# Another tabled order of the instructions of an attention and MoE kernel

## The chip, the core and the metric

The kernel runs on one core of a Trainium2 chip. The metric is the device time of one execution in microseconds (us); less is better. Shown times are of executions without disturbance.

## What is computed

For batch B = 4, heads H = 8, S = 576 positions and head size D = 64, all in float32; `k` and `z_prev` come scaled by 8.

```python
scores = scale * np.matmul(q, k.transpose(0, 1, 3, 2))     # scale = 1/sqrt(D)
scores = np.where(causal, -1000000000.0, scores)
a = np.exp(scores - scores.max(-1, keepdims=True))
a /= a.sum(-1, keepdims=True) + 1e-09
local = np.matmul(a, v)
q_p = phi(q)                      # x + 1 above zero, exp(x) below
mem_out = (q_p @ M_prev) / (q_p . z_prev + 1e-06)
g = 1 / (1 + np.exp(-beta))
x = g * mem_out + (1 - g) * local          # then [2304 tokens, 512]
h = np.maximum(np.maximum(x @ w1, x @ w2), x @ w3)   # [2304, 768]
return h @ w_out                                      # [2304, 512]
```

## The kernel before

The tokens of each batch are cut into two halves, of 320 and 256 rows. A half of a batch with two of its heads is a pair; there are 32 of them, the 16 of the first half first. When the four pairs of a half and batch are done, its tokens go through the MoE part.

For a pair, `load_qk` and `load_v` fetch the inputs (`rk`, `rw` for q and k, `rv` for v, `mv` for the memory). Matmuls take float32 numbers as a high part and a low part in a faster format: `split_q` and `split_k` cast the high part (`qs`, `k` from `rk` or `rw`; on ScalarE or VectorE) and subtract it for the low part (on VectorE or GpSimd). `product` multiplies them on TensorE into one of two PSUM banks, `bs`, which holds one block of scores at a time. `masked` on VectorE reads the bank, adds the causal mask, writes `p` and leaves the least value in `st` (in the trace a CUSTOM_DVE instruction and a read of its accumulator; in the order an ISA instruction); then the bank is free for the next `product`. `exponential` is ScalarE's (`p` from `p` and `st`, sum in `sum`), `turned` makes the reciprocal of the sum on VectorE, `normal` scales `p` on GpSimd. `phi` makes the memory's part (`phe`, `phf`, with the norm `nn`). The blocks of `p` are turned on TensorE into the banks `bt` and copied to `pt` (ScalarE or VectorE) in the first part of the kernel; later VectorE's STREAM_TRANSPOSE turns them in pieces that go to DRAM and come back into `pt` with DMAs. `values` multiplies `pt` with `mv` and `rv` into the bank `bv`, whose result is split into `xh` and `xl`.

`moe_up` multiplies `xh` and `xl` with the three weights' parts `wh`, `wl` into three banks `bm` (three matmuls a product); the greatest of the three is kept in `t` (copy, then VectorE's maxima) and split into `hh` and `hl` (`hhr`, `hlr` for the last 64 of 320 tokens). `moe_down` multiplies with `woh`, `wol`. The weights themselves are split in the first 100 us (`load_weights`: ScalarE, VectorE, and a subtract on GpSimd or VectorE that writes `wl`).

All these instructions are not issued as written but noted in a list, in the order of the program; an instruction that may run on either of two engines is noted with both. `Plan.emit` then issues them in the order that the table `ORDER` gives: each word is a place in the list of what is still to be issued, `b` takes the second engine, and `+n` puts n filler matmuls ahead, which read the mask and write a bank of no use at that time. Each engine runs its own instructions in the order of issue, and waits on others by semaphores that follow from the data. So the table sets what stands in front of what on each of the engines. The table has 5431 words, 13 of them with fillers (119 matmuls) and 205 with `b`. The names in the traces carry L259 (the line in `emit` that issues) for all instructions, and L254 for the fillers.

Of the kernel before, what the change touches and what calls it, by code (L numbers as in the profile page):

```python
# [23 lines left out]
class Half:  # L24
# [27 lines left out]

ORDER = """
    2 0 1 0 0 0 2 15 15 15 4 3 2 1 21+30 22+12 21 21 0 17 15 140 82 10 79 78 77 13 76 6 12 12 18+9 17 17 9 0
    19+10 0 27 0 17 8 6 23 0 16 39+12 5 20 15 34 34 51 33 13 7 34 34 1 0 15 6 2 28 16+6 8 5 5 24 6 2 20 1 0 9
    9 9 31+16 0 8 2 1 3 21 25 106 11+4 1 23 4 9 4 26+2 38 38 8b 1 65 3 23 10 3 1 8 19 7 19 4+6 0 5 3 28 28 50
    8 1 10 2 10 0 31 17 65 14 14 21 63 27 4 4 3 11 57 22 15 23+8 21 30 50 21 143 21 15 11 19 19b 2 21 20 13 18
    39 21 5 2 129 11 11 2 16 17 3 3 5 11 1 11 9 14+1 6 13b 13 0 9 1 109 108 7 18 27 7b 25 8 100 24 0 0 5 21 39  # L60
    5 5 5+3 6 90 5 21 16 0 31 19 1 0 26 25 11 79 2 11 52 14 271 271 0 20 35 36 13 13 8 32 36 17 11 30 31 31 20
    9 3 9 17 25 13 35 16 34 8 16 48 8 20 14 20 8 10 18 7 128 7 10 28 15 125 15 26b 8 19 19 9 18 8 8 58 6 15 3
    34 6 32 15 13 19 49 104 17 28 76 100 0 2 11 11 3 12 3 9 91 26 10 37 25 52 51 9 14 23 17 46 4 184 28 28 22
    2 31 15 39b 3 29 31 19 24 41 17 22 17 6 2 29 29 29 33 32 29 38 37 1 21 14 9 10 132 24b 8 11 23 17 1 8 11 9
    23 23 23 8 11 15 20 50 11 21 133 21b 7 1 9 16 9 16 34 53 23 2 31 121 31 8 8 118 2 16 16 12 14 5 11 27 6
    103 88 4 25 10 9 1 17 50 48 30 31 21 28 44 28 46 22 17 26 3 40 29 29 37b 25 6 19 11 59 17 33 60 32 58 26 1
    11 32 10 69 51 31 21 27 48 28 29 2 82 21 10 25 12 15 10 2 10 20 227 20 20 21 20 37 8 19b 9 12 18 218 31 2
# [3 lines left out]
    31 20 6 28 28 19 27 35 35 35 35 35 35 35 14 34 2 5 12 15 2 19b 1 10 21 25 18 24 7 9 3 17 20 20 62 78 39 20  # L71
    75 75 63 60 61 25 3 24 3 15 22 55 22 22 7 62 65 99 2 97 2 60 1 245 13 58 17 1 1 52 51 15 15 15 15 15 39b
    15 78 77 67 0 66 14 0 72 9 7 16 109 32 62 16 16 65 0 30 7 28 9 74 13 13 13 13 3 12 5 20 1 10 43 10 10 10
    195 78 4 77 9 78 48 48 1b 0b 13 3 19 43 68 0 1 1 70 11 29 65 11 3b 13 13 13 13 13 13 55 13 13 19 9 12 12
    12 24 9 11 72 71 45 72 71 22 31 43b 75 9 16 347 29 29 19 28 1 11 11 8 11 8 133 31 22 22 22 10 12 12 19 19
    19 19 19 14 18 86 40 85b 42 316 40 14 39 39 39 156 115 9 308 16 113 20 13 11 1 11 2 107 5 14 14 68b 10 67
    13 13 46 13 13 134 62 13 85 13 9 6 11 11 8 10 92 10 53 90 76 76 88 53 17 113 80 111 86 0 73 16 82 1b 71 5
    103b 11b 7 0b 76 1 0 1 0 10 10 10 10 10 10 10 10 10 10 10 10 10 117 82 121 115 115 116 10 7 50 113 113 13
    13 13 13 108b 13 13 13 13 3 70 3b 50 0 6 9 38 0 95 8 8 8 63 33 9 8 60 88 89 5 11 3 85 57 64 10 10 26 51 1
    3 4 50 50 22 21 237 237 21 7 7 45 7 7 7 7 7 7 7 7 2 83 83 84 83 159 10 8b 82 0b 80 2 32 32 32 17 17 17 147  # L80
    17 1 7 15 45 1 14 14 14 14 196 9 13 13 13 104 6 148 35 12 8 145 6 139 98 13 10 10 92 7 6 13 13 13 13 4 131
    87 5 1 10 166 10 10 10 10 10 36 76 10 6 9 123 117 122 151 9 34 15 10 14 14 14 14 14 14 14 6 42 13 4 107
    58b 107 5 7 130 1 9 9 55 1 93 8 8 126 122 125 5 2 6 47 11 120 46 84 46b 11 85 4 8 12 12 12 12 12 12 12 12
    12 1 11 11 3 30 10 110 107 108 62 1 107 9 102 102 0 102 94 13 5 12 97 12 12 12 12 93b 95 7 1 93 92 4 4 91
    90 83 83 88 89 88 88 88 4 4 13 47 76 43 43 42 41 36 37 35 37 35 34 34 113 107 113 112 107 105 105 108 112
    112 34 17 17 17 17 17 17 17 104 27 27 57 4 12 25 4 97 57b 57 4 4 4 4 4 4 273 72 132 5 4 130 104 17 17 264
    102 104 252 255 251 21 21 39 3 121 20 1 62 42 36 41 15 71 90 15 17 17 86 143 4 147 36 142 149 36 105 4 4
    34 12 48b 4 4 101 101 56 133 75 31 31 31 31 4 4 2 49 88 88 53 49 121b 247 52 381 246 86 64 44 4 41 1b 40 4
    25 369 1 37b 24 19 75 1 22 263 22 22 364 3 3 3 19 18 15 31 31 31 255 177 17 30 30 17 15 25 2 2 2 2 12 207
    14 14 159 2 2 73 234 74b 25 13 12 12 12 12 2 2 10 2 32 32 143 317 2 2 60 5 37 37 29 56 6 6 34 34 53 53 52  # L90
# [24 lines left out]
    1 68 49 50 6 2 48 70 171 63 64 65 65 99 66 5 5 376b 168 62 152 152 152 159 5 151 161 9 9 5 5 5 89 89 5 52
    152 19 51 6 189 6 6 6 15 6 14 14 14 161 6 6 6 6 6 9 9 9 20 6 8 8 6 16 7 122 176b 7 41 14 25 25 114 55 161
# [1100 lines left out]
```

## Time and profile before

| | us |
|---|---|
| median of 3 runs | 478.63 |
| lowest and highest | 478.06, 479.09 |
| the profiled execution | 477.99 |
| its span on the core | 476.2 |
| TensorE busy | 464.3 |
| VectorE busy | 369.1 |
| ScalarE busy | 256.7 |
| GpSimd busy | 280.5 |

The span runs from the first instruction to the last; the time of the execution has 1.79 us around it. TensorE's granted clock is the full one, 9 tenths or more, in all of the 40 slices of the page. Busy times of one engine are sums over its instructions; a TensorE that is busy may still run below its peak, since matmuls overlap and their ends are modelled.

### The profile page before, as it was taken

Reading aid. Unit: us, or ns where it says so; the run is one execution under the profiler, and the core shown is the slowest. Engines: PE = TensorE matmul, PEld = TensorE weight load, DVE = VectorE, ACT = ScalarE, POOL = GpSimd, SP = SyncE. Lnnn points to the kernel's source line nnn. Section 1 sums busy time; section 2 is a strip of 40 time slices with the busy share of each in tenths; the row PEclk is TensorE's granted clock in tenths of the full one; section 3 lists DMA queues with packets and bytes.
Section 4 is the critical chain, followed back from the end, with each engine's and each line's share of the span. In section 5 each row is a group of like instructions: output and inputs, shape, how many; then the busy total and the mean of one; then the engine's idle time right before and its main releaser. Section 6 shows DMA issues by size and latency. Waiting matters only on the chain. (4 is left out here: it accounts for less than half of the span.)

```text
span 476.2 us, 10470 instructions
## 1 busy us (share of the span) xinstructions
PE 464.3 (98%) x3321; PEld 402.7 (85%) x3321; DVE 369.1 (78%) x1205; ACT 256.7 (54%) x725; POOL 280.5 (59%) x433
## 2 busy tenths in 40 slices
PE   8898999999999999999999999999999999999997
PEld 7556878778998789997989878998998889987996
DVE  3899999987979898888889887788788878831231
ACT  5898978775565545445564364554636544421001
POOL 4787878785575846554566676677657556430100
PEclk9999999999999999999999999999999999999999
DMA  6788979755558768789979989899898798666001
GB/s 160 189 240 242 274 224 260 204 102 146 126 144 185 194 185 218 203 201 267 221 225 240 235 221 274 240 272 276 198 271 244 186 232 256 181 189 142 1 1 45
DMA packets 147255, 94.22 MB, mean 198 GB/s; under 512 B 99968, under 2 KB 126848, under 8 KB 147200
## 3 DMA queue, kind: packets, MB, share of 16 engines
q1 hardware_dynamic: 146384, 93.36, 74.5%
q8 instruction: 26, 0.43, 0.4%
q14 instruction: 29, 0.24, 0.2%
q10 hardware_dynamic: 816, 0.20, 0.2%
HBM read 61.94 MB, written 31.59 MB: 196 GB/s over the span
## 5 line engine op out<-in xcount | busy, mean ns | idle before, releaser
L259 PE MATMUL bm<-xh,wh 128*128 128x320 f32 (+1 forms) x576 | 167.1, 305 | 0.3 <-DVE t L259 0.3
L259 PE MATMUL bm<-xl,wh 128*128 128x320 f32 (+1 forms) x576 | 165.8, 298 | 0.0
L259 PE MATMUL bm<-xh,wl 128*128 128x320 f32 (+1 forms) x576 | 162.3, 297 | 0.0
L259 POOL TENSOR_SCALAR p<-p,sum,gb 128x576 f32<-128x576 f32 (+3 forms) x128 | 87.3, 687 | 63.4 <-DVE sum L259 49.5
L259 ACT ACTIVATE p<-p,st 128x320 f32<-128x320 f32 (+4 forms) x144 | 84.1, 584 | 60.5 <-DVE st L259 41.3
L259 PEld LDWEIGHTS bm<-xh,wh 128*128 128x128 f32 x576 | 106.9, 189 | 6.5 <-DVE t L259 1.9
L259 PEld LDWEIGHTS bm<-xl,wh 128*128 128x128 f32 x576 | 107.7, 189 | 1.8 <-issue 0.3
L259 PEld LDWEIGHTS bm<-xh,wl 128*128 128x128 f32 x576 | 106.6, 189 | 1.2 <-issue 0.2
L259 DVE TENSOR_TENSOR t<-bm,t 128x320 f32<-128x320 f32 (+1 forms) x96 | 43.4, 453 | 39.1 <-PE bm L259 24.1
L259 DVE CUSTOM_DVE_ANT_0 p<-bs,mask 128x192 f32<-128x192 f32 (+3 forms) x128 | 59.6, 474 | 15.9 <-PE bs L259 14.6
L259 PE MATMUL bs<-k,qs 128*128 128x288 f32 (+5 forms) x264 | 67.1, 312 | 3.6 <-DVE st L259 3.0
L259 DVE STREAM_TRANSPOSE rk<-p 128x512 f32<-128x512 f32 (+2 forms) x80 | 57.6, 729 | 5.1 <-POOL p L259 4.8
L259 PEld LDWEIGHTS bs<-k,qs 128*128 128x128 f32 (+1 forms) x264 | 44.3, 186 | 9.7 <-DVE st L259 4.0
L259 POOL TENSOR_TENSOR p<-phf,nn 128x128 f32<-128x128 f32 (+1 forms) x96 | 36.7, 390 | 20.3 <-DVE nn L259 14.6
L259 PE MATMUL bv<-pt,rv 128*64 128x256 f32 (+1 forms) x384 | 40.4, 344 | 0.0
L259 PEld LDWEIGHTS bv<-pt,rv 128*64 128x64 f32 x384 | 27.4, 137 | 14.6 <-issue 0.2
L259 PE MATMUL bm<-wol,hh 128*128 128x512 f32 (+1 forms) x102 | 39.3, 387 | 0.0
L259 PE MATMUL bm<-woh,hh 128*128 128x512 f32 (+1 forms) x102 | 38.8, 385 | 0.0
L259 PE MATMUL bm<-woh,hl 128*128 128x512 f32 (+1 forms) x102 | 38.7, 381 | 0.0
L259 POOL TENSOR_TENSOR phe<-phf,z 128x384 f32<-128x384 f32 (+1 forms) x32 | 28.9, 902 | 16.0 <-DVE phf L259 5.7
L259 POOL TENSOR_TENSOR xl<-kt,xh 128x256 fp32r<-128x256 f32 (+1 forms) x28 | 22.4, 803 | 23.1 <-ACT kt L259 23.1
L259 ACT COPY t<-bm 128x320 f32<-128x320 f32 (+1 forms) x38 | 15.3, 402 | 30.8 <-PE bm L259 21.4
(102 smaller groups left out, 810.8 us busy)
## 6 DMA issues: line engine op xcount, KB each, us to landing
dp<-rk SPq DMA_DIRECT2D x16, 1024.0 KB, 5.7
pt<-dp SPq DMA_DIRECT2D x64, 256.0 KB, 4.8
rw<-in_moe_w_dram SPq DMA_DIRECT2D x18, 512.0 KB, 4.9
dh<-rk SPq DMA_DIRECT2D x6, 704.0 KB, 3.7
pt<-dh SPq DMA_DIRECT2D x24, 176.0 KB, 3.5
rw<-dq SPq DMA_DIRECT2D x32, 128.0 KB, 3.8
rv<-in_v_dram SPq DMA_DIRECT2D x32, 128.0 KB, 4.7
out_dram<-g SPq DMA_DIRECT2D x15, 256.0 KB, 4.3
```

The lines of the kernel that those rows point to most:

```text
L259: getattr(getattr(self.nc, self.ENGINES[eng]), name)(**kw)
```

## The change

The table `ORDER` is replaced. It is another one from the second word on, with the same number of words. Nothing that is noted changes: the computed values, tiles, banks, DMAs and the instructions are the same ones. A constant `BANK` is added that nothing reads; it moves the lines of the kernel by six, so that L259 becomes L265 and L254 becomes L260.

```diff
+BANK = (((0, 512),),)
+
 ORDER = """
-    2 0 1 0 0 0 2 15 15 15 4 3 2 1 21+30 22+12 21 21 0 17 15 140 82 10 79 78 77 13 76 6 12 12 18+9 17 17 9 0
...
+    2 34+30 1 2 0 0 0 5 4 3 2 0 11 0 23+12 22 10 144 18 17 16 15 15 75 10 77 15b 20+9 19 72 72 10 0 17 21+10 0
...
```

Counted from the two tables: the fillers go from 119 in 13 groups to 100 in 11; the words with `b` from 205 to 234. Fifteen copies and casts go from ScalarE to VectorE and 14 subtracts from VectorE to GpSimd, as the sums of both kinds: VectorE's subtracts for `k` from `rk` fall from 30 to 20 and those for `qs` from `rw` from 17 to 12, GpSimd's rise from 14 to 24 and from 15 to 20; VectorE's casts of `hh` go from 12 to 18, those of `qs` from `rw` from 6 to 10. The number of waits of TensorE for other engines is 506 before and 502 after.

Where a piece of the order stands, the names are those of the tiles with their numbers. Between the matmuls that run at 140 and 205 us in the trace of before, GpSimd has 61 instructions in the old order and 80 in the new; the subtracts among them (for `k`, `qs`, `xl`, `hlr`) are 10 and 26.

*Near 222 us, VectorE.* The `masked` of a block of 288 rows of scores in the bank `bs0`; the old order:

```order
L259 CAST qs_96<-rw_126 128x256
L259 STREAM_TRANSPOSE rk_89<-rk_89 128x8x2x32
L259 STREAM_TRANSPOSE rk_89<-rw_126 128x256
L259 TENSOR_TENSOR qs_96<-rw_126,qs_96 128x256 x2
L259 TENSOR_TENSOR hl_79<-t1_103,hh_78 128x256
L259 ISA p_97,st_98<-bs0_116,mask_62 128x288
L259 ISA st_98 128x1
L259 ISA p_97,st_98<-bs1_117,mask_62,st_98 128x288
```

The new order, the same `masked` (the first ISA) and what is behind it:

```order
L265 TENSOR_TENSOR k1_2_84<-rw_126,k1_2_84 64x320
L265 TENSOR_REDUCE nn0_100<-phe0_86 128x4
L265 TENSOR_TENSOR t1_103<-bm2_123,t1_103 128x320
L265 ISA p_97,st_98<-bs0_116,mask_62 128x288
L265 ISA st_98 128x1
L265 CAST k1_2_84<-rk_89 64x256
L265 ISA p_97,st_98<-bs1_117,mask_62,st_98 128x288
L265 ISA st_98 128x1
L265 SCALAR_TENSOR_TENSOR phf1_88<-phe0_86,phf1_88 128x256
L265 TENSOR_SCALAR sum_99<-sum_99 128x1
L265 TENSOR_TENSOR k1_2_84<-rk_89,k1_2_84 64x256
```

The two subtracts of `qs` and the `hl` subtract stood directly ahead of the `masked`; now a subtract of `k`, a norm and a maximum do.

*Near 222 us, TensorE.* What stands ahead of the next scores matmul into that bank (448 columns); the old order:

```order
L259 MATMUL bm2_123<-wol_73,hh_78 128x512
L259 MATMUL bm0_121<-xh1_75,wl0_69 128x320
L259 MATMUL bm2_123<-woh_72,hh_78 128x512
L259 MATMUL bm2_123<-woh_72,hl_79 128x512
L259 MATMUL bs0_116<-k1_0_82,qs_96 128x448
```

The new order:

```order
L265 MATMUL bm2_123<-woh_72,hl_79 128x512
L265 MATMUL bm2_123<-wol_73,hh_78 128x512
L265 MATMUL bv0_120<-pt_129,mv1_93 64x64 x2
L265 MATMUL bv0_120<-pt_129,mv1_93 64x256 x2
L265 MATMUL bv0_120<-pt_129,rv1_95 64x256 x2
L265 MATMUL bv0_120<-pt_129,rv1_95 64x128 x2
L265 MATMUL bs1_117<-k1_1_83,qs_96 128x448 x2
L265 MATMUL bs0_116<-k1_0_82,qs_96 128x448 x2
```

The product of the values of a pair and two scores matmuls of the other bank came in between.

*Near 200 us, VectorE.* The `masked` of 448 rows in the bank `bs1`; the old order:

```order
L259 CAST k1_3_85<-rw_126 64x320
L259 TENSOR_TENSOR t1_103<-bm2_123,t1_103 128x320
L259 STREAM_TRANSPOSE rk_89<-p_97 128x5x4x32
L259 TENSOR_TENSOR k1_3_85<-rw_126,k1_3_85 64x320
L259 ISA p_97,st_98<-bs1_117,mask_62 128x448
L259 ISA st_98 128x1
```

The new order:

```order
L265 TENSOR_TENSOR t0_102<-bm2_123,t0_102 128x320
L265 STREAM_TRANSPOSE rk_89<-p_97 128x6x4x32
L265 TENSOR_TENSOR nn0_100<-nn0_100,gb_63 128x4
L265 ISA p_97,st_98<-bs1_117,mask_62 128x448
L265 ISA st_98 128x1
L265 SCALAR_TENSOR_TENSOR phf1_88<-phe0_86,phf1_88 128x256
```

The subtract of `k` ahead of the `masked` is gone from there; a product of the norm stands in its place.

*Near 61 us, VectorE.* The `masked` of 320 rows in `bs1` beside a `phf`; the old order:

```order
L259 TENSOR_SCALAR bm1_122<-bm1_122 128x512
L259 ISA p_97,st_98<-bs0_116,mask_62 128x192
L259 ISA st_98 128x1
L259 SCALAR_TENSOR_TENSOR phf1_88<-phe0_86,phf1_88 128x384
L259 SCALAR_TENSOR_TENSOR g1_128<-rw_126,bm1_122 128x512
L259 ISA p_97,st_98<-bs1_117,mask_62 128x320
L259 ISA st_98 128x1
```

The new order:

```order
L265 TENSOR_SCALAR bm1_122<-bm1_122 128x512
L265 SCALAR_TENSOR_TENSOR g1_128<-rw_126,bm1_122 128x512
L265 ISA p_97,st_98<-bs1_117,mask_62 128x320
L265 ISA st_98 128x1
L265 RECIPROCAL nn0_100<-nn0_100 128x6
L265 ISA p_97,st_98<-bs0_116,mask_62 128x192
L265 ISA st_98 128x1
L265 TENSOR_TENSOR hlr_81<-t0_102,hhr_80 128x64
L265 SCALAR_TENSOR_TENSOR phf1_88<-phe0_86,phf1_88 128x384
```

The `masked` of `bs1` went ahead of the `phf`, and the two blocks of scores changed places.

## Rows read from the trace of the kernel before

**Rows 1.** The page's busy times: engine, us, share of the span, instructions.

```profile
PE 464.3 (98%) x3321; PEld 402.7 (85%) x3321; DVE 369.1 (78%) x1205; ACT 256.7 (54%) x725; POOL 280.5 (59%) x433
```

**Rows 2.** Windows by stage: stretch, length, busy us by engine, clock, DMA share, GB/s.

```profile
23.00:100.00 77.00, 74.51 (x508) 56.39 (x509) 73.17 (x232) 66.41 (x189) 60.38 (x94) 1.00 0.83 231
...
140.00:205.00 65.00, 63.21 (x429) 56.62 (x427) 57.52 (x192) 33.07 (x99) 37.21 (x62) 1.00 0.76 194
205.00:250.00 45.00, 43.69 (x289) 38.70 (x285) 39.52 (x124) 25.13 (x69) 25.54 (x35) 1.00 0.88 230
250.00:440.00 190.00, 189.82 (x1384) 167.58 (x1381) 143.59 (x472) 88.57 (x244) 113.06 (x161) 1.00 0.87 229
```

**Rows 3.** TensorE's largest waits: for whom; us in total, times, longest.

```profile
PE bs L259 <- DVE st L259: 3.6, 7, 1.1
PE bt L259 <- ACT pt L259: 1.6, 4, 0.8
PE bt L259 <- ACT p L259: 1.3, 1, 1.3
```

**Rows 4.** Chain of waits, its last long piece: start, us, what.

```profile
439.41 33.76 PE bm L259 x263
```

**Rows 5.** Timeline at 222 us: start, us, engine, operation, idle time before and releaser.

```profile
220.31 1.25 DVE L259 TENSOR_TENSOR qs<-rw,qs 128x256 fp32r<-128x256 f32 x2
...
221.82 0.45 DVE L259 CUSTOM_DVE_ANT_0 p<-bs,mask 128x288 f32<-128x288 f32 x1
...
219.51 1.44 POOL L259 TENSOR_TENSOR qs<-rw,qs 128x256 fp32r<-128x256 f32 x2 [0.22 <-DMA mv<-in_v_dram]
...
222.41 0.44 PE L259 MATMUL bs<-k,qs 128*128 128x448 f32 x1 [1.10 <-DVE st L259]
```

**Rows 6.** Timeline at 200 us, VectorE, GpSimd and TensorE.

```profile
198.38 1.22 DVE L259 TENSOR_TENSOR k<-rw,k 64x320 fp32r<-64x320 f32 x1
199.63 0.63 DVE L259 CUSTOM_DVE_ANT_0 p<-bs,mask 128x448 f32<-128x448 f32 x1
...
198.38 0.87 POOL L259 TENSOR_TENSOR xl<-kt,xh 128x320 fp32r<-128x320 f32 x1
...
200.32 0.53 PE L259 MATMUL bs<-k,qs 128*128 128x288 f32 x2 [0.56 <-DVE st L259]
```

**Rows 7.** Timeline at 58 to 61 us, VectorE, GpSimd and TensorE.

```profile
58.22 1.69 DVE L259 SCALAR_TENSOR_TENSOR phf<-phe,phf 128x384 f32<-128x384 f32 x1
...
58.20 1.29 POOL L259 TENSOR_TENSOR wl<-g,wh 128x512 fp32r<-128x512 f32 x1
...
60.98 0.81 PE L259 MATMUL bs<-rk 64*128 64x192 f32 x4 [0.58 <-DVE st L259]
```

**Rows 8.** Timeline of TensorE at four further waits.

```profile
44.94 0.74 PE L259 MATMUL bt<-ident,p 128*128 128x128 f32 x5 [0.83 <-ACT pt L259]
...
176.62 0.30 PE L259 MATMUL bs<-k,qs 128*128 128x64 f32 x1 [0.56 <-DVE k L259]
...
155.11 0.41 PE L259 MATMUL bs<-k,qs 128*128 128x320 f32 x1 [0.33 <-DVE st L259]
...
151.72 0.30 PE L259 MATMUL bs<-k,qs 128*128 128x64 f32 x1 [0.34 <-DVE st L259]
```

**Rows 9.** Timeline of TensorE in the start: fillers, then a wait.

```profile
16.39 0.61 PE L254 MATMUL bm<-mask 128*128 128x128 bf16 x8
...
18.26 0.47 PE L259 MATMUL bt<-ident,rk 80*128 80x80 f32 x4 [1.26 <-ACT p L259]
```

**Rows 10.** Tiles k and qs: subtracts, ns least/median/most, first and last start, shape.

```profile
L259 DVE TENSOR_TENSOR k<-rw,k x10: 485/778/1219, 185.7 to 402.0; 64x320 fp32r<-64x320 f32 x10
...
L259 POOL TENSOR_TENSOR k<-rw,k x22: 858/876/979, 182.0 to 399.1; 64x320 fp32r<-64x320 f32 x22
...
L259 DVE TENSOR_TENSOR qs<-rk,qs x15: 484/489/1230, 108.2 to 173.6; 64x320 fp32r<-64x320 f32 x15
...
L259 POOL TENSOR_TENSOR qs<-rk,qs x9: 862/879/1012, 110.7 to 172.3; 64x320 fp32r<-64x320 f32 x9
```

More of the change, by code (lines that the diff above doesn't have):

```diff
@@ L61 @@
[L61 to L65, printed above, removed]
@@ L74 @@
[L74 to L78, printed above, removed]
@@ new lines @@
+    16 8 0 14 7 24 15 23 45 7 0 13 41 41 35+1 9 0 0 50 5 32 10 30 7 29 19+4 3 18 7 12 24 25b 16 17 6 11 6
+    37+13 13 6 4 27 5 31 31 7 3 14+6 34 2 33 3 6 6 24 71 0 9b 1 4 36 4 6 11+7 9 0 20 30 0 20 19 56 7 4 4 4 28
+    28 0 0 8 75 0 19 4 22 4 14 1 13 27 59 26 25 8 18 4 11 11 54 54 53 52 20 21+6 22 20 14 19 23 24 2 21 20 13
+    23 17 102 3 5 11 18 0 10 13 4 6 14 8 12 2 12 11 5 3 11 9b 31 10 29 4 10 27 103 9 17 4 8 9+2 97 10 7 2 4 6
+    23 0 22 33 288 4b 0 3 46 46 83 282 0 8 8 8 42 24 25 17 9 14 20 21 15 24 24 4 18 30 67 33 30 8 12 28 22 27
@@ new lines @@
+    3 3 3 59 285 5 169 156 3 4 279 1b 73 164 37 2 0 9 47 122 200 199 199 1 20 20 151 254 254 20 20 20 41 139
+    249 171 331 149 166b 10 10 185 40 39 18 162 115 55 10 10 16 10 8 104 1 1 1 1 1 1 231 0b 7 2 6 143 144 143
+    141 2 5 2 7 7 92 7 219 7 1 87 87 6 104 113 280 14 14 14 6 378 242 500 109 241 3 3 11 4 10 10 268b 4 4 4
+    198 198 198 91 73 73 73 185 193 88 192 354 2 254b 2 245 182 182 90 90 90 29 29 244b 30 29 29 29 30 29 2 2
+    2 13 13 24 13 13 13 13 172 13 13 13 158 441 66 67 98 371 165 165 206 98 158 206 213b 64 363b 206 206 2 2
@@ new lines @@
+    155 206 204b 203b 309 184 308 309 308 157 155 6 200 200 194 16 83b 191 6 152 177 2 5 5 5 5 2 18 4 2 292
+    224 142 142 222 181 3 6 6 6 6 173 175 175 2 2 4 4 21 4 4 166b 388 385 384 384 6 6 2 5 5 378 5 3 264 375
+    198 160 211 26 26 259 4 25 207 4 4 191 154 33 140 23 145 248 145 9 9 9 9 9 9 9 9 9 9 105 236 137b 173 238
+    239 137 128 234 236 4 4 4 253 102 4 4 165 0 1b 223 223 2 57 0 117 1 1 217 157 53 0 120 10 52 51 51 51 51
+    51 52 51 110b 110 108 1 1 1 1 1 5 5 16 134 134 5 5 140 1 131 1 12 12 1 92 90 90 89 1 196 197b 446 10 128 1
@@ new lines @@
+    9 4 4 58 57 7 13 7 4 123 123 6 153 175 153 122 173 10 6 9 163b 6 20 20 6 165 119 6 163 18 113 113 18 197
+    156 155b 157 139 139 114 6 6 6 6 6 6 23 23 23 6 22 6 6 4 134 253b 3 7 7 7 7 134 170 171 4 1 5 5 5 166 18
+    18 117 18 228 18 5 3 16 118 166 118b 16 16 16 4 15 15 15 112 15 99 19 6 6 142 142 213 6 6 11 104 138 6 6
+    66 6 6 6 21 202 137 62 94b 6 94 61 196 20 20 20 21 20 21 20 53 84 120 21 20 23 23 23 33 117 8 8 8 8 72 71
+    29 161 67 64 169b 19 166b 16b 106 106 164 62 18 18 18 18 18 18 21 156b 8 315 143 141 141 8 8 8 8 8 49 12
@@ L206 @@
+    20 0 0 18 18 18 18 18 0 17 17 20 0 0b 0 0 0 0 11 11 0 0 0 0 0 0 0 0 3b 27 27 27 27 27 27 27 27 0 0b 1 1 1
+    1 1 1 1 1 2 2 2 2 2 0b 1 1 1 1 1 6 1 1 4 4 0 3 3 0 0b 0 0 0 0 0 0 2 2 2 2 2 2 0 1 1 1 1 1 1 0 0 0 0 0 0 3
+    0 0 0 0 0 0 0 0 0 0 0 0 0 0 0 0 0 0 0 0 0 0
 """
```

263 lines of the change are left out of this document (130 added, 133 removed), and 6 rows, old and new, of the table ORDER.

## The prediction

> **What bounds the kernel now.** I read the page's busy table first, then the windows by stage, then what TensorE waited for, then the end of the chain of waits, and last the timeline around the largest waits. The busy table [rows 1] shows TensorE busy for 464.3 of 476.2 us; VectorE follows with 78%, GpSimd with 59%. The windows [rows 2] show where the rest is: from 250 to 440 us TensorE is busy for 189.82 of 190 us while VectorE has work for 143.59 (76%); from 140 to 205 us it is short by 1.79 us while VectorE has work for 57.52 of 65 (88%), from 205 to 250 us by 1.31, and from 23 to 100 us, where the weights are split and VectorE is 95% busy, by 2.49. So TensorE loses time where VectorE is nearly full, and a reordering can win there only. The chain [rows 4] ends in 33.76 us of plain up and down matmuls, whose order the change leaves nearly alone.
>
> The largest waits [rows 3] are of one kind: a scores matmul (`bs`) waits until VectorE has read that bank with `masked` (its maximum lands in `st`): 3.6 us in 7 pieces. Next are `bt` transposes that wait for a ScalarE copy (`pt`, 1.6 us in 4) and one that waits for an exponential in the start (1.3 us). Those three lines hold 6.5 us; that, and the further waits on single operands [rows 8], is all that moving instructions can fetch outside the stretch of the weights.
>
> **The change part by part.** No operation is added or removed but 19 filler matmuls in the start; what changes is places and, for some casts, copies and subtracts, the engine. So the sum is made of the waits whose cause moves away, less what the new places cost.
>
> *At 222.41 us* the scores matmul waited 1.10 us [rows 5]. VectorE ran two subtracts of `qs` in 1.25 us (the first shares its time with GpSimd's two of the same kind, 1.44 us from 219.51) and an `hl` subtract, and only then, at 221.82, the `masked` of 0.45 us that frees the bank. In the changed order 23 matmuls lie between the place of that `masked` and the scores matmul, instead of 6, and the two `qs` subtracts stand behind it. What is late next is ScalarE's cast of `qs`, with two matmuls of cover: a loss of a few tenths at most, which I leave to what comes back below. I take 1.10 as gone.
>
> *At 200.32 us* the wait was 0.56 us [rows 6]. VectorE's subtract of `k` took 1.22 us beside a GpSimd subtract (0.87 us from the same moment), against 0.485 at its best [rows 10], and `masked` started only at 199.63. The changed order has no subtract there: a transpose and a small product stand ahead of the `masked`, and between the matmul that fills the bank and the one that waits for it stand ten matmuls. At 189.82 us for 1384 matmuls [rows 2], 0.137 us each, that is 1.4 us of cover for a `masked` of 0.63. Gone: 0.56.
>
> *At 60.98 us* the wait was 0.58 us [rows 7]: VectorE's `phf` took 1.69 us beside a GpSimd weight subtract of 1.29 us that had started 0.02 us before, with a `masked` behind it. In the changed order the `masked` stands ahead of `phf`, and twelve matmuls (1.6 us) cover it. Gone: 0.58. The `phf` itself may be as long as before, but behind it stands nothing that TensorE waits for in the next few matmuls.
>
> *Four smaller ones* [rows 8]: at 44.94 us (0.83, a copy behind ScalarE's weight activation, which itself waited for a DMA), eight matmuls stand between copy and transpose where one stood; at 176.62 (0.56) the `k` subtract is done long before, and a `qs` subtract with five matmuls of cover is the last to come; at 155.11 (0.33) the `masked` has sixteen matmuls of cover where it had four; at 151.72 (0.34) the bank is free long before, and a cast on ScalarE with fifteen matmuls of cover comes last. Together 2.06.
>
> The sum of what is relieved is 1.10 + 0.56 + 0.58 + 2.06 = 4.30 us.
>
> *What comes back.* TensorE has 502 waits on other engines in the changed order against 506, at the same distribution of distances. VectorE's work is the same by my count (subtracts that leave it for GpSimd, 14 at some 0.45 us, are paid for by copies and casts that come from ScalarE, 15), so its share in 140 to 205 us stays near 88%, and at that share a queue of in-order work makes some operation late somewhere [rows 2]. I cannot name the places, so I bound it: from 0 (every new place has cover) to all 4.30 (the waits only move). I take half, 2.15: the relieved places have cover of 0.7 to 3 us (five to 23 matmuls), which speaks for a gain, but VectorE is as full as before, which speaks for new waits elsewhere, and no row decides between the two.
>
> *The fillers.* 19 fewer at 0.61 us for 8 [rows 9] are 1.45 us of TensorE's time at most. They stood where TensorE would have waited anyway: behind the eight of 16.39 us TensorE still waits 1.26 us for ScalarE's exponential. Taking away a filler only lengthens such a wait. Cost and gain: nothing, with bounds 0 and -1.45; nearest row: the wait of 1.26, so 0.
>
> *The moved subtracts.* What the rows show: a VectorE subtract of `qs` takes between 0.484 and 1.230 us, one of `k` between 0.485 and 1.219, and the same ones on GpSimd 0.879 and 0.876 in the median [rows 10]; the long VectorE cases are those that meet a GpSimd operation [rows 5, 6, 7]. Fourteen subtracts more on GpSimd mean 14 x (0.88 - 0.49) = 5.5 us more of time in which a VectorE subtract cannot run at its best. I count it at nothing in the sum, because VectorE has 14 such instructions fewer that could be hit, and I keep it as a rival below. The Trainium skill, page "SBUF — State Buffer", section "SBUF: two separate sides", states the rule behind these rows: the port pair that VectorE and GpSimd share is a lock, which whichever starts first holds for its whole instruction while the other stands still. By it every subtract that goes to GpSimd, where it lasts longer, lengthens the time in which the pair is taken, so the rule speaks against this part of the change; the trace agrees on the lock (1.219 against 0.485). By the rule alone the 5.5 us would all fall on VectorE, and the sum would be between 477.99 - 2.15 and 477.99 - 2.15 + 5.5.
>
> Sum on the profiled execution (477.99 us, of which 476.2 is its span): 477.99 - 4.30 + 2.15 = 475.84. The median of the runs is 478.63, 0.64 above it; so 478.63 - 2.15 = 476.48, rounded to 476.5.
>
> **The rivals.** *All of the relief stays, and the weights' stretch gains too.* For it: nearly all of 250 to 440 us runs without a wait [rows 2], so an order without them exists where VectorE is at 76%; and in 23 to 100 us, where VectorE is the bound, a `phf` that does not have to stand beside 1.29 us of GpSimd [rows 7] gives up to that back. Against it: by my count of both orders, with the mean duration of each kind of instruction, the VectorE work that is issued ahead of the same point of TensorE's work is within 0.2 us of what it was up to 60 us. Price: -4.30 and one such `phf`, -1.29: 478.63 - 5.6 = 473.0.
>
> *The waits only move.* For it: the same count of waits, the same VectorE share. Against it: three of the seven places were not thin but hit by the meeting of VectorE and GpSimd, and those meetings are what moved. Time: 478.6, within 0.9.
>
> *GpSimd holds VectorE up between 140 and 205 us.* By the order, the instructions between the matmuls that run at 140 and 205 us today are 80 on GpSimd instead of 61, and its subtracts among them 26 instead of 10. At 37.21 us for 62 [rows 2] the 19 are 11.4 us: GpSimd would be at 48.6 of 65 us, 75% instead of 57%. The 16 subtracts hold the shared time for 16 x 0.88 instead of 16 x 0.49, 6.2 us more; VectorE has 7.5 us to spare there (65 - 57.52). It decides when more than that falls on VectorE. The price goes by the waits of today: those that `masked` or `k` ended in this stretch sum to 0.56 + 0.56 + 0.33 + 0.34 = 1.8 us at 10 subtracts; at 26 they would be 4.7, 2.9 more. The three places outside the stretch (1.10 + 0.58 + 0.83 = 2.5) still give half of their relief, -1.25. So 478.63 + 2.9 - 1.25 = 480.3, slower than before.
>
> **How the numbers follow.** Forecast (a part of the relief stays, 475.0 to 477.6): 0.42. All of it stays and more (472.5 to 475.0): 0.20. The waits only move (477.7 to 479.5): 0.17. GpSimd holds VectorE up (479.6 to 482): 0.21. A measurement of this kernel can tell about 0.2%, 0.96 us, from no change: faster is below 477.67, slower above 479.59. Faster 0.62, same 0.17, slower 0.21. The range holds the forecast, the better case but for what lies below its price, and the slower case up to its price: 473.0 to 480.5.
>
> **What would show it.** Right: TensorE's waits on `st` fall from 3.6 us to 2 or less, no scores matmul waits a whole microsecond, and 140 to 250 us of TensorE's work take 1.5 us less; GpSimd's share there rises without longer VectorE subtracts. Wrong on the fillers: the end of the first scores comes more than 1 us earlier. Wrong by the slower rival: VectorE's `k` and `qs` subtracts have medians near 0.8 us and `bs` waits in the place of work that now starts later. Wrong in the other direction: VectorE's busy time between 23 and 100 us falls by more than 1 us and all later work starts that much earlier.

## The result, and the profile after

The new order takes 471.3 us (median of 4 runs, 470.8 to 472.0) against 478.5 on the same chip: a ratio of 0.985 (95% interval 0.9833 to 0.9867), 7.2 us less. The forecast was 476.5 with a range down to 473.0, so the direction was right, and the time lies 1.7 us below the range. The profiled execution after takes 471.96 us, with a span of 470.1.

The page's busy times, which answer [rows 1]:

```profile
PE 462.5 (98%) x3302; PEld 401.8 (85%) x3302; DVE 359.3 (76%) x1206; ACT 252.8 (54%) x710; POOL 292.8 (62%) x447
```

The windows, which answer [rows 2] (length, then busy us of TensorE, weight loads, VectorE, ScalarE, GpSimd, then clock, DMA share, GB/s):

```profile
23.00:100.00 77.00, 74.80 (x508) 57.19 (x507) 68.79 (x221) 65.44 (x187) 61.25 (x94) 1.00 0.87 231
...
140.00:205.00 65.00, 65.00 (x444) 58.95 (x443) 55.41 (x186) 37.63 (x110) 50.10 (x81) 1.00 0.84 224
205.00:250.00 45.00, 44.92 (x300) 40.19 (x299) 36.79 (x132) 22.74 (x62) 28.71 (x40) 1.00 0.92 243
250.00:440.00 190.00, 189.77 (x1387) 167.86 (x1387) 139.74 (x459) 82.98 (x224) 107.41 (x151) 1.00 0.83 217
```

From 140 to 205 us TensorE is busy without a gap, and does 444 matmuls where it did 429. GpSimd has 50.10 us of work there (77%; the prediction worked out 75%), and VectorE has less than before, not more. From 23 to 100 us VectorE's busy time is 4.4 us lower at the same length of window, but for 221 instructions where it had 232; in this trace TensorE waits for a load there (the first of the waits further down). A second trace of the new order has no such wait, and 2.6 us less for 230:

```profile
23.00:100.00 77.00, 76.39 (x519) 58.40 (x518) 70.59 (x230) 67.33 (x191) 62.98 (x97) 1.00 0.86 230
```

TensorE's waits of the whole span, which answer [rows 3] (for whom; us in total, times, longest):

```profile
PE bv L265 <- DMA rv<-in_v_dram: 1.1, 1, 1.1
PE bm L265 <- DVE t L265: 0.8, 2, 0.6
PE bt L265 <- POOL wl L265: 0.5, 1, 0.5
```

The waits for `st` are gone from the largest. The same view of the stretch behind the weights alone, first 116 to 260 us of before, then 116 to 250 us of after:

```profile
PE bs L259 <- DVE st L259: 3.0, 6, 1.1
PE bs L259 <- DVE k L259: 0.6, 1, 0.6
```

```profile
PE bm L265 <- DVE t L265: 0.8, 2, 0.6
```

The three places of the prediction, in the timeline of after (which answers [rows 5 to 7]): the `masked` of the bank of 222 us and, four microseconds later, the scores matmuls that follow without a wait; the `masked` of 200 us and its scores matmul; and the `masked` and the `phf` of 61 us, the scores matmul behind them, and GpSimd's subtract.

```profile
208.50 0.45 DVE L265 CUSTOM_DVE_ANT_0 p<-bs,mask 128x288 f32<-128x288 f32 x1
...
212.49 1.09 PE L265 MATMUL bs<-k,qs 128*128 128x448 f32 x4
...
186.73 0.62 DVE L265 CUSTOM_DVE_ANT_0 p<-bs,mask 128x448 f32<-128x448 f32 x1
...
187.48 0.42 PE L265 MATMUL bs<-k,qs 128*128 128x288 f32 x2
...
57.74 0.48 DVE L265 CUSTOM_DVE_ANT_0 p<-bs,mask 128x320 f32<-128x320 f32 x1
...
58.63 0.55 DVE L265 SCALAR_TENSOR_TENSOR phf<-phe,phf 128x384 f32<-128x384 f32 x1
...
59.32 0.59 PE L265 MATMUL bs<-rk 64*128 64x192 f32 x3
...
57.12 1.29 POOL L265 TENSOR_TENSOR wl<-g,wh 128x512 fp32r<-128x512 f32 x1
```

None of the three scores matmuls waits. The `phf` takes 0.55 us and not 1.69, since GpSimd's subtract ends at 58.41, before it starts.

**Where the time went.** To lay traces side by side I gave each matmul the usual distance from its start to the next start of its kind (the median in the trace of before: 0.147 us for 320 columns, 0.231 for 512, 0.120 for 256). What a kernel needs to reach a given sum of these, less the sum, is what TensorE has lost by then; fillers count as lost. How the kinds are cut moves the lost columns by some us, and a gain by at most 0.5.

| work done by TensorE, us | before | after | gain in the stretch |
|---|---|---|---|
| 20 (at 33 us) | 13.63 | 13.33 | 0.30 |
| 80 (at 98 to 100 us) | 20.09 | 17.61 | 2.18 |
| 120 (at 139 to 141 us) | 21.21 | 19.20 | -0.47 |
| 220 (at 241 to 247 us) | 27.27 | 20.96 | 4.30 |
| 443 (end) | 29.71 | 23.66 | -0.26 |

These two executions differ by 6.0 us (477.99 and 471.96), not by the 7.2 of the medians. The gain has two parts: 2 to 2.5 us while the weights are split, and some 4 us between 140 and 250 us. The sums of the prediction for these were 0.7 (half of 0.58 + 0.83) and 1.45 (half of 1.10 + 0.56 + 0.56 + 0.33 + 0.34).

### The profile page after: what moved, and what is told of

Same layout as the page of the kernel before. It is cut to its first block, busy times and chain, and to the rows that moved or that the text cites. A ratio compares the mean times of both kernels' runs of the same rounds, so it can differ in the third digit from the quotient of the medians.

```text
span 470.1 us, 10417 instructions
## 1 busy us (share of the span) xinstructions
PE 462.5 (98%) x3302; PEld 401.8 (85%) x3302; DVE 359.3 (76%) x1206; ACT 252.8 (54%) x710; POOL 292.8 (62%) x447
## 4 chain that ended last, share of the span: by engine, by line
PE 90%; DMA 3%; DVE 2%; ACT 2%; SPq 1%; issue 1%; ACTq 0%; DVEq 0%
PE bm L265 62%; PE bv L265 11%; PE bs L265 10%; PE bt L265 5%; PE bm L260 2%; DMA rk<-in_q_dram 2%; DMA rw<-dq 2%; SPq L265 1%; DVE p L265 1%; ACT pt L265 0%; DVE qs L265 0%; ACT p L265 0%; DVE rk L265 0%; DVE t L265 0%; ACT rk L265 0%
## 5 line engine op out<-in xcount | busy, mean ns | idle before, releaser
L265 PE MATMUL bm<-xh,wh 128*128 128x320 f32 (+1 forms) x576 | 167.1, 305 | 1.1 <-DVE t L265 0.8
L265 PE MATMUL bm<-xl,wh 128*128 128x320 f32 (+1 forms) x576 | 166.5, 299 | 0.1
L265 PE MATMUL bm<-xh,wl 128*128 128x320 f32 (+1 forms) x576 | 162.7, 299 | 0.0
L265 POOL TENSOR_SCALAR p<-p,sum,gb 128x192 f32<-128x192 f32 (+3 forms) x128 | 89.5, 703 | 46.8 <-DVE sum L265 39.7
L265 PEld LDWEIGHTS bm<-xh,wh 128*128 128x128 f32 x576 | 106.6, 189 | 8.0 <-DVE t L265 2.4
L265 ACT ACTIVATE p<-p,st 128x448 f32<-128x448 f32 (+4 forms) x144 | 84.1, 585 | 48.8 <-DVE st L265 32.4
L265 PEld LDWEIGHTS bm<-xl,wh 128*128 128x128 f32 x576 | 107.7, 189 | 1.8 <-issue 0.3
L265 PEld LDWEIGHTS bm<-xh,wl 128*128 128x128 f32 x576 | 106.3, 189 | 2.2 <-issue 1.1
L265 DVE CUSTOM_DVE_ANT_0 p<-bs,mask 128x320 f32<-128x320 f32 (+3 forms) x128 | 59.2, 473 | 13.0 <-PE bs L265 11.1
L265 PE MATMUL bs<-k,qs 128*128 128x288 f32 (+5 forms) x264 | 66.4, 309 | 0.3 <-DVE qs L265 0.2
L265 DVE TENSOR_TENSOR t<-bm,t 128x320 f32<-128x320 f32 (+1 forms) x96 | 43.4, 452 | 29.1 <-PE bm L265 25.3
L265 DVE STREAM_TRANSPOSE rk<-p 128x512 f32<-128x512 f32 (+2 forms) x80 | 57.4, 728 | 5.7 <-POOL p L265 5.3
L265 POOL TENSOR_TENSOR p<-phf,nn 128x128 f32<-128x128 f32 (+1 forms) x96 | 37.9, 401 | 21.9 <-DVE nn L265 8.1
L265 PEld LDWEIGHTS bs<-k,qs 128*128 128x128 f32 (+1 forms) x264 | 44.5, 186 | 3.9 <-DVE st L265 0.5
L265 POOL TENSOR_TENSOR phe<-phf,z 128x384 f32<-128x384 f32 (+1 forms) x32 | 28.4, 886 | 25.4 <-DVE phf L265 10.9
L265 POOL TENSOR_TENSOR hl<-t,hh 128x256 fp32r<-128x256 f32 x31 | 23.3, 753 | 30.5 <-DVE hh L265 20.7
L265 PE MATMUL bv<-pt,rv 128*64 128x256 f32 (+1 forms) x384 | 41.1, 344 | 1.1 <-DMA rv<-in_v_dram 1.1
L265 PEld LDWEIGHTS bv<-pt,rv 128*64 128x64 f32 x384 | 27.8, 137 | 16.4 <-DMA rv<-in_v_dram 1.6
L265 PE MATMUL bm<-woh,hh 128*128 128x512 f32 (+1 forms) x102 | 38.9, 388 | 0.0
L265 PE MATMUL bm<-wol,hh 128*128 128x512 f32 (+1 forms) x102 | 38.9, 383 | 0.0
L265 PE MATMUL bm<-woh,hl 128*128 128x512 f32 (+1 forms) x102 | 38.7, 383 | 0.0
L265 ACT COPY t<-bm 128x320 f32<-128x320 f32 (+1 forms) x33 | 13.2, 401 | 44.0 <-PE bm L265 34.1
```

Of the source, the lines that this page charges most:

```text
L265: getattr(getattr(self.nc, self.ENGINES[eng]), name)(**kw)
```

## The experiments

In all kernels the same instructions are noted, and only the table differs (and the constant that nothing reads); line numbers move with its length. The diffs show the order of instructions, cut to what moves.

**Which stretch gains.** Three mixed orders: the new one up to a switch and the old one after it, or the other way round.

```diff
-order = old
+order = new[:1387] + [i for i in old if i not in new[:1387]]
```

> The first 1387 words in the new order, all that is left in the old order (the switch lies at the matmul that runs near 116 to 118 us). From the two traces TensorE gains 2.4 us on the old order by the time that it has done the first 100 us of its work, and 3.9 more later. If the two gains are independent (theory 1), this kernel keeps the first: 478.5 - 2.4 = 476.1. If the later gain follows from the lead of the first stretch (rival: what is done earlier gives every later wait its slack), most of the later waits go too: 473 or less.

Measured: 477.1 us, ratio 0.997 (0.9946 to 0.9995).

```diff
-order = old
+order = old[:1378] + [i for i in new if i not in old[:1378]]
```

> The first 1378 words in the old order, all that is left in the new order. Theory 1 (independent gains): the later part alone, 478.5 - 4 = 474.5. Rival (lead of the first stretch): nearly nothing, 477.5 or more.

Measured: 476.95 us, ratio 0.9971 (0.9953 to 0.9989). So by the medians either half alone brings 1.4 to 1.6 us, together 3 of 7.2. The interval of the first (0.2 to 2.6 us less) still holds the 2.4 of theory 1, that of the second (0.5 to 2.2) does not hold its 4. By the accounts of the traces both theories miss a piece. From 120 us of work to the end the first kernel loses 8.55 us, as the old order does (8.50), and the second 5.00, as the new one does (4.46). Each stretch goes as its own order goes, which is theory 1. But between 100 and 120 us of work, behind the switch, they lose 2.1 and 2.6 us where old and new lose 0.8 and 1.2. My reading is that the second half's queues find the other half's state. The second kernel's waits from 116 to 146 us:

```profile
PE bm L261 <- DVE t L261: 1.9, 2, 1.3
PE bm L261 <- ACT t L261: 0.6, 1, 0.6
```

The up matmuls wait there for the maxima (`t`). A switch at 250 us tells whether that cost is one of switching at any place:

```diff
-order = old
+order = new[:3058] + [i for i in old if i not in new[:3058]]
```

> The new order up to the matmul of 250 us, what is left in the old order. If the gain is all made before 250 us and the rest of either order is as good (theory 1 with the switch where VectorE has room, so that it costs little): 471 to 472.5. If the new order's last part is worth something, or the switch costs as much as at 118 us (1.3 to 1.9 us): 473 or more.

Measured: 471.7 us, ratio 0.9843 (0.9809 to 0.9876), beside 471.0 for the new order on the same chip. So the gain is made before 250 us, but for less than the intervals can tell, and a switch there, where VectorE has work for 76% of the time [rows 2], costs nothing that shows. That VectorE's room is the reason was not tested.

**Whether waits come back.** Three `masked` go ahead in the old order, each by one to four instructions; nothing else changes, and VectorE's long subtracts stay beside GpSimd's. VectorE's order near 222 us, and in the same way near 200 and 61 us:

```diff
+ISA p_97,st_98<-bs0_116,mask_62 128x288
 STREAM_TRANSPOSE rk_89<-rw_126 128x256
 TENSOR_TENSOR qs_96<-rw_126,qs_96 128x256 x2
 TENSOR_TENSOR hl_79<-t1_103,hh_78 128x256
-ISA p_97,st_98<-bs0_116,mask_62 128x288
```

> The old order with three instructions moved, each a VectorE read of a scores bank: ahead of the two qs subtracts and the transpose (the wait at 222.41 us), ahead of the k subtract (200.32) and ahead of the phf (60.98). The meetings of VectorE and GpSimd there stay as they are. Theory 3 (a wait whose cause is moved away is gone, nothing comes back, and each costs what the matmul starts late, 0.16 us more than its listed idle time): 478.5 - (1.25 + 0.71 + 0.74) = 475.8. The prediction's half given back: 478.5 - 2.24 / 2 = 477.4. Rival (the waits only move): 478.5.

Measured: 475.5 us (12 runs), ratio 0.9949 (0.9932 to 0.9966), 2.6 us less than before, with an interval of 1.6 to 3.3: as much as the late starts of the three places (2.70) or their listed waits (2.24) with nothing given back, and more than half of either. In the timeline of this kernel (VectorE, then TensorE, first at 222 us of before, then at 61):

```profile
218.30 0.41 DVE L257 CUSTOM_DVE_ANT_0 p<-bs,mask 128x288 f32<-128x288 f32 x1
...
219.02 0.86 DVE L257 TENSOR_TENSOR qs<-rw,qs 128x256 fp32r<-128x256 f32 x2
...
219.22 0.40 PE L257 MATMUL bm<-woh,hl 128*128 128x512 f32 x1
219.45 0.37 PE L257 MATMUL bs<-k,qs 128*128 128x448 f32 x1
...
58.61 1.28 DVE L257 SCALAR_TENSOR_TENSOR phf<-phe,phf 128x384 f32<-128x384 f32 x1
...
60.31 0.59 PE L257 MATMUL bs<-rk 64*128 64x192 f32 x3
```

The scores matmul follows its neighbour at 0.23 us, although the two subtracts of `qs` stand where they stood. The `phf` still stands beside GpSimd and takes 1.28 us, and no matmul waits for it. So at these places no meeting had to be taken apart; it was enough that the `masked` did not stand behind it.

TensorE's order is the same in both kernels, so each matmul can be compared with itself in the two traces. The lead on the old order goes from 0.01 to 0.67 us at the place of 60.98, from 1.11 to 1.67 at 200.32 and from 1.71 to 3.03 at 222.41; by 240 us it is back at 2.62, and it ends at 2.6. Behind 140 us the two moves thus kept 1.5 of the 1.96 us of their late starts: most of it, not all. The 0.4 us between 67 and 180 us came where nothing was moved, so that the total comes so near to 2.70 is in part luck.

The same with four waits of the new order, three of them in the weights' stretch:

```diff
 DMA rv0_94<-in_v_dram 128x2x64
+DMA rv0_94<-in_v_dram 128x2x64
 DMA rk_89<-in_k_dram 80x4x64
...
-DMA rv0_94<-in_v_dram 128x2x64
```

> The new order with four moves for its own largest waits: the second half of a values load (rv) issued behind its first (wait of 1.14 us at 32.54), a weight activation behind the cast of xh (0.37 at 35.17), a phi activation behind two copies to pt (0.48 at 37.24), and a maximum of three ahead of a reciprocal and a copy (0.61 at 129.62). Late starts listed by pitch: 1.52 + 0.53 + 0.55 + 0.77 = 3.4. Theory 3 (nothing comes back): 471.3 - 3.4 = 467.9. In the weights' stretch VectorE is the bound, so it may give back the first three: 471.3 - 0.8 = 470.5.

Measured: 471.2 us, ratio 0.9851 (0.9822 to 0.9881): no gain that shows. TensorE's list of waits has two others in their place:

```profile
PE bt L263 <- ACT pt L263: 1.5, 2, 1.2
PE bt L263 <- POOL p L263: 1.0, 1, 1.0
```

At 33.43 and 36.02 us two transposes wait now, for GpSimd and ScalarE, 1.18 and 1.49 us by late starts, where the three waits taken away had 2.6. This looks as if in this stretch the waits only move, as a rival of the prediction had it, but it is not shown: the largest of the three, 1.5 us for the load of `rv`, stands in the first trace of the new order and is missing in a second one of the same table, so the move may have had nothing to take away. Four moves of VectorE's instructions behind 120 us instead, run twice, the second time beside the new order:

```diff
 ISA p_97,st_98<-bs0_116,mask_62 128x288
+TENSOR_TENSOR qs_96<-rw_126,qs_96 128x256
 TENSOR_SCALAR sum_99<-sum_99 128x1
 RECIPROCAL sum_99<-sum_99 128x1
 TENSOR_SCALAR sum_99<-sum_99 128x1
-TENSOR_TENSOR qs_96<-rw_126,qs_96 128x256
```

> The new order with four moves on VectorE, all behind 120 us: a maximum of three ahead of a norm's sum (late start of 0.77 us at 129.62), a masked ahead of a cast (0.25 at 205.40), a qs subtract ahead of three small sums (0.35 at 378.76), a k subtract ahead of a transpose (0.20 at 397.07). Theory 3 (where TensorE is the bound, what is taken away stays away): 471.3 - 1.57 = 469.7. Rival (the new order has no room left; each move makes another operation late): 471 to 472.

> The new order unchanged, on the same chip as the next: its time for the comparison with the four late moves, 471.3. Both have the same words up to 118 us.

> The four late moves once more, beside the new order on the same chip. By the traces of the first run TensorE's work behind 140 us loses 0.95 us less than in the new order, against 0.80 by late starts, and the move at 129.62 gave nothing. So 0.9 less than the run before it: 470.4 if that is 471.3. If the moves give nothing: the same.

Measured: the first time 471.9 us, with runs from 468.3 to 473.2, too wide to tell 1.6 us from nothing. The second time 469.6 us (469.2 to 470.0), ratio to before 0.9801 (0.9775 to 0.9826), beside 471.0 (469.8 to 471.7) and 0.9828 for the new order: 1.4 us less. By the traces the three moves behind 200 us keep what they took (from 140 us of work to the end 3.4 us lost against 4.4); the wait at 129.62 is still there at 129.18, 0.48 us late where it was 0.77, and the stretch around it gains nothing. It is the fastest version, by less than the two intervals can tell apart.

**What VectorE loses to GpSimd while the weights are split.** One `phf` goes one instruction ahead in the old order, so that it starts before GpSimd's subtract of the weights; then three of VectorE's instructions that met GpSimd so: this `phf`, a cast of `hh` and an `hlr` subtract.

```diff
+SCALAR_TENSOR_TENSOR phf1_88<-phe0_86,phf1_88 128x384
 ISA p_97,st_98<-bs0_116,mask_62 128x192
 ISA st_98 128x1
-SCALAR_TENSOR_TENSOR phf1_88<-phe0_86,phf1_88 128x384
```

> The old order with one move: VectorE's phf of 58.22 us goes one instruction ahead, so that it starts at 57.95, before GpSimd's weight subtract of 58.20 and not 0.02 us after it. Theory 6 (in the weights' stretch, where VectorE is 95% busy, what VectorE stands still behind GpSimd lies on the path): phf takes 0.5 to 0.6 us instead of 1.69, GpSimd's subtract some 0.3 longer, and the wait of 60.98 us (0.74 by late start) goes with it: 478.1 - 0.8 to -1.3 = 476.8 to 477.3. Rival (there it is the loads or another engine that set the pace; one place more or less moves a wait): 478.1, and the wait comes back within 20 us.

> The old order with three VectorE instructions of the weights' stretch put one to two places ahead, so that each starts before the GpSimd instruction that it met: phf at 58.22 (1.69 us), a cast of hh at 63.32 (0.79) and an hlr subtract at 84.47 (0.82). They lose 1.1 + 0.5 + 0.6 = 2.2 us of standing still. Theory 6 (there VectorE's time is on the path): 478.2 - 1 to 2.2 = 476.0 to 477.2. Rival (other engines and loads set the pace there): 478.2, with VectorE waiting for others instead.

Measured: with one 477.6 us, ratio 0.999 (0.9974 to 1.0005), which does not tell 1 us from nothing; and with three 477.55 us against 478.8, ratio 0.9967 (0.9947 to 0.9987), 1.2 us less, inside theory 6 at its lower half. The pair at 58 us in the timeline of the second, VectorE's row and GpSimd's:

```profile
57.92 0.59 DVE L257 SCALAR_TENSOR_TENSOR phf<-phe,phf 128x384 f32<-128x384 f32 x1
...
58.17 1.49 POOL L257 TENSOR_TENSOR wl<-g,wh 128x512 fp32r<-128x512 f32 x1
```

The `phf` starts 0.25 us before GpSimd's subtract and takes 0.59 us, where it took 1.69 when it came 0.02 us after it [rows 7]; GpSimd pays 0.2 us. The Trainium skill, page "SBUF — State Buffer", section "SBUF: two separate sides", says that of a VectorE instruction with two inputs there and a GpSimd instruction that reads it, whichever starts first has the shared port pair for its whole instruction. Both traces agree, and they show that the turn is worth 1.1 us to VectorE and costs GpSimd 0.2.

What this was worth to TensorE is another matter. Matmul by matmul, the lead of the kernel with three on the old order goes from 0.01 to 0.67 us at the place of 60.98. That is as much as the moved `masked` alone gave in the kernel above, where the `phf` stayed at 1.28 us. It does not change where the cast stood (63.32), and it rises from 0.82 to 1.36 where the `hlr` subtract stood (84.47); 0.2 of this shows in the two other kernels with moves in the old order as well. So about 1.0 us came back of the 2.0 that VectorE won at the three places, and the larger part of that is the wait for `st`. That VectorE's time by itself lies on the path here, as theory 6 says, is not shown.

**Places or engines.** The new places with the old engines, the old places with the new engines, and the two kinds apart (245 instructions differ: 100 subtracts, 145 copies and casts).

```diff
-order = new
+order = [(place in new, engine of old)]
```

> The new order with every instruction on the engine on which the old order had it: 245 instructions go back. If the places make the gain (theory 2), most of it stays: 471.5 to 474. If it is the moved subtracts, casts and copies (rival), it goes: 476.5 or more. A third way: the new places hold only for the engines they were made with, and the queues clash: 478 or more, with waits in new places; then neither part is worth anything alone.

> The old order with every instruction on the engine on which the new order has it. Theory 2 (the places): no gain, 478 to 481, since the queues of the old order are filled with other instructions than those that they were made for. Rival (the engines): 473 to 475. By the sum of the prediction, GpSimd's extra holding of VectorE would show here as longer subtracts and scores matmuls that wait, up to 5.5 us: 484.

> The new order with all 100 subtracts that differ between VectorE and GpSimd (57 one way, 43 the other) on the engine of the old order. Theory 5 (a table of places holds for the engines that it was made with, each change costs some): the 20 of the earlier run cost 2.1, 100 would cost up to 10; with the 145 copies and casts of the next run it adds to the 13.6 of all 245, so 475 to 481. Rival (GpSimd's hold): the new order loses less or gains, 471 or below.

> The new order with all 145 copies and casts that differ between ScalarE and VectorE (80 one way, 65 the other) on the engine of the old order, subtracts as in the new one. Theory 5: 471.3 plus what is left of 13.6 after the run before, 475 to 481. If only the subtracts matter, 471 to 473.

> The new order, with the 20 subtracts between 140 and 205 us that the new table gives to GpSimd and the old one gave to VectorE back on VectorE, in their places. Rival of the prediction (GpSimd's longer hold costs VectorE): faster, by up to 20 x 0.25 = 5 us, 466 to 470. Theory 4 (VectorE's room is what counts: it has 65 - 55.4 = 9.6 us free there, and 20 subtracts take 9 to 10.7): VectorE becomes full, scores matmuls and maxima wait, 474 or more.

| kernel | us | ratio to before (95%) |
|---|---|---|
| new places, old engines | 484.9 | 1.0139 (1.0123 to 1.0154) |
| old places, new engines | 496.8 | 1.0396 (1.0362 to 1.0431) |
| new, 100 subtracts on old engines | 478.8 | 1.0017 (0.9997 to 1.0038) |
| new, 145 copies and casts on old engines | 478.6 | 1.0006 (0.9991 to 1.0021) |
| new, 20 subtracts of 140 to 205 us back on VectorE | 473.4 | 0.9911 (0.988 to 0.9943) |

Neither part is worth anything alone, the third way that the expectation named: new places with old engines lose 13.6 us on the new order, old places with new engines 18.3 on the old. The two kinds of engine choice, put back one at a time, cost 7.5 and 7.3, together 14.8, about the 13.6 of both. The other two ways, places or engines alone, are both refuted. What counts against my slower rival is the last row: with fewer of these subtracts on GpSimd the kernel is 2.1 us slower, not up to 5 faster. Its windows (VectorE is the third busy time, GpSimd the fifth):

```profile
140.00:205.00 65.00, 63.91 (x431) 56.86 (x429) 59.18 (x198) 35.74 (x104) 37.83 (x59) 1.00 0.83 219
```

GpSimd is back at 37.83 us, VectorE goes from 55.41 to 59.18, and TensorE loses 1.1 us in the stretch, with waits of up matmuls for the maxima (`t`) on top of its list. VectorE is at 91% there, not full as theory 4 had it.

What VectorE's instructions would take at the quick fifth of their kind (operation, tiles and shape, over the traces of before and after), and what they took beyond that, over the whole span:

| kernel | at the quick fifth, us | beyond it, us | time, us |
|---|---|---|---|
| before | 403.4 | 31.8 | 478.5 |
| after | 402.6 | 23.6 | 471.3 |
| new, 20 subtracts back on VectorE | 410.2 | 24.0 | 473.4 |
| new, 145 copies and casts on old engines | 397.5 | 23.2 | 478.6 |

With the 20 subtracts back VectorE's instructions are no shorter beside a GpSimd with less to do; there is only more work. And the last row says that VectorE's work and delays alone do not set the time: it has the least of both and gains nothing.

**The fillers.** The new order without its 100 fillers; in the table each `+n` goes, here in its first line:

```diff
-    2 34+30 1 2 0 0 0 5 4 3 2 0 11 0 23+12 22 10 144 18 17 16 15 15 75 10 77 15b 20+9 19 72 72 10 0 17 21+10 0
...
+    2 34 1 2 0 0 0 5 4 3 2 0 11 0 23 22 10 144 18 17 16 15 15 75 10 77 15b 20 19 72 72 10 0 17 21 0 16 8 0 14 7
...
```

> The new order without its 100 filler matmuls; no result changes. If they stand where TensorE waits anyway and do nothing else, 471.3. If they lie on the path, 471.3 - 100 x 0.066 = 464.7. If TensorE's granted clock falls without them, the clock row of the page shows the lower level in the start, and the time is 473 or more.

Measured: 471.45 us, ratio 0.9848 (0.9813 to 0.9883), the same as with them. The row of the page with TensorE's granted clock in 40 slices, and the largest wait:

```profile
PEclk9999999999999999999999999999999999999999
```

```profile
PE bt L263 <- DMA rk<-in_q_dram: 4.8, 2, 2.9
```

TensorE waits 4.8 us for the first loads instead of doing fillers, the clock is at 9 tenths or more in every slice, and the end doesn't move.

## Why the prediction was wrong, step by step

**What bounds the kernel: right.** TensorE lost time where VectorE was nearly full, and what was gained was gained there, before 250 us (the switch at 250 us). Behind it the two traces differ by 0.26 us.

**The places: right.** All seven waits of [rows 5 to 8] are gone in the new order. The three `masked` of the first three places stand where the order put them, and moving them alone gave 2.6 us; for the four smaller waits the reasons are read from the order and were not tested one by one.

**The half that comes back: wrong, and the largest error.** I took half of 4.30 us as given back, with no row for it; the reason was that VectorE is as full as before. It is not quite: from 140 to 205 us it has work for 85% of the time, where it had 88%. And behind 140 us little came back. The six late starts of before in that stretch (0.50 + 0.50 + 0.72 + 0.71 + 1.25 at the places of the prediction, and 0.37 at 246.19) sum to 4.05, and TensorE gained 4.30 there, where the sum had 1.45. The only late start of more than 0.2 us in this stretch of after is one of 0.25, at 205.40. The kernel with three moves kept 1.5 of 1.96 us there. My reading, which no run tests by itself: a `masked` needs 0.5 to 0.6 us somewhere in 1.4 us or more of cover, and at 85% VectorE has that. Whether the half would have been fair in the weights' stretch is not settled by the four moves. One wait between the two stretches did come back: at 127.12 us of before TensorE started 0.65 us late for `st`, and at 129.62 us of after 0.77 late for `t`.

**The size of a wait: too small by 0.16 us each.** The two rows of TensorE ahead of the wait at 222.41 us of before [rows 5]:

```profile
220.69 0.40 PE L259 MATMUL bm<-woh,hh 128*128 128x512 f32 x1
220.93 0.39 PE L259 MATMUL bm<-woh,hl 128*128 128x512 f32 x1
```

The matmul of 220.93 lasts 0.39 us, so the list counts idle time from 221.32. But matmuls overlap: the one before it was followed after 0.24, and the next could have started at 221.16. The late start is 1.25 us, not 1.10. For the six places behind 140 us that is 3.1 us listed and 4.05 late; the prediction left one of them out (0.21 listed, at 246.19).

**The weights' stretch: missed.** I had 0.58 + 0.83, halved, and kept one long `phf` as part of a rival. By the two traces it gained 2.2 us between 20 and 80 us of TensorE's work, and the sign that the prediction named for it came: VectorE's busy time there fell by more than 1 us. The trace of before had more to show: VectorE, 95% busy there, stood still behind GpSimd in nine instructions, some 3.5 us in all (each against the quick fifth of its kind), and in the new order in two, 0.5 us. Three of the nine, taken away in the old order, gave 1.2 us, of which 0.66 is the wait at 60.98 that the sum had as 0.58. What the others are worth, and so the rest of this stretch's gain, is not settled, for one trace can't tell: traces whose words are the same up to 116 us had lost between 14.9 and 18.9 us at 80 us of work. Part of this is when the first loads land. The kernel with one `phf` moved shows such a wait, of 2.1 us at 32.61 us, which the old order does not have in its own trace:

```profile
PE bt L257 <- DMA rk<-in_k_dram: 2.1, 1, 2.1
```

**The moved subtracts: right that they cost nothing; the slower rival, at 0.21, did not come.** With 20 of them back on VectorE the kernel is even 2.1 us slower. GpSimd's share went to 77%, near the 75% worked out, but VectorE's subtracts got no longer. The two rows that answer [rows 10]:

```profile
L265 DVE TENSOR_TENSOR qs<-rk,qs x15: 484/486/1207, 103.5 to 166.9; 64x320 fp32r<-64x320 f32 x15
...
L265 DVE TENSOR_TENSOR k<-rw,k x12: 484/486/651, 192.3 to 392.8; 64x320 fp32r<-64x320 f32 x12
```

The subtracts of `k` from `rw` have a median of 0.486 us where they had 0.778. The count that VectorE's work stays the same was right (0.8 us less at the quick fifth), but its instructions took 8.2 us less beyond that, although GpSimd was busier (292.8 us where it was 280.5). So more of GpSimd's time beside VectorE did not mean more time lost. The bound of +5.5 us multiplied durations without asking which of the two starts first, and that the order sets.

**The fillers: right.** No change without any.

**The sum put right.** 478.5 - 4.05 (late starts behind 140 us) - 1.73 (those at 44.94 and 60.98, 0.99 and 0.74), with nothing given back, would have given 472.7. The 1.4 us that lack to 471.3 stay open: 1.2 of them are not in this pair of traces, which differ by 6.0 us. The rival "all of the relief stays, and the weights' stretch gains too" (473.0) came nearest in kind, with a chance of 0.20, but its band of 472.5 to 475.0 does not hold 471.3 either: it took the seven waits by their listed size, 0.16 us too small each, and with it the lower end of the range was 1.1 us too high from this alone.

## What to carry to other kernels

Count a wait of TensorE by how late its matmul starts against the usual distance of its kind, not by the idle time that is listed; and take a wait that is moved under cover as mostly gone where TensorE, the waiting engine, is the bound (1.5 of 1.96 us stayed away here). Whether it only moves where another engine is the bound stayed open. Where a second engine is nearly full, look for its instructions that last longer than the quick ones of their kind, and first at those with something behind them that the bound engine waits for. An order and a choice of engines are one thing: in this kernel taking either from the new table without the other cost more than both bring.

## What the runs showed of the hardware

Where VectorE's `phf` and GpSimd's subtract of the weights meet, the order of their starts decides the price: 0.02 us late cost VectorE 1.1 us, 0.25 us early cost GpSimd 0.2. Not every VectorE instruction pays it: in the new order a `masked`, which reads a PSUM bank and the mask, starts at 57.74 us in the middle of such a subtract and takes its usual 0.48 us. Fillers had no effect on TensorE's granted clock here: 9 tenths or more in all slices, although TensorE's first 23 us hold 17.25 us of busy time without them and 21.70 with them. And the first 100 us of this kernel differ between traces of the same order by up to 4 us, in part by when loads land, so that a gain there is read from medians only.
